# PSUM banks of the attention stage granted one by one, with new engine orders

## The chip, the cores and the metric

The kernel runs on one NeuronCore of one Trainium2 chip. The metric is the device time of one execution in microseconds (us), taken over several runs. The profile comes from one further execution.

## The reference

What has to be computed, in three parts that feed one another (the constants are those of this case):

```python
# q, k, v: (2 batches, 12 heads, 448 tokens, 64)
scores = q @ k.T / 8;  scores = where(above the diagonal, -1e9, scores)
e = exp(scores - rowmax(scores));  attn = e / (rowsum(e) + 1e-9)
x = (attn @ v) laid out as (896 tokens, 768)
h = x @ w_in                                   # 768 -> 2048
g = where(h > 0, h, exp(min(h, 0)) - 1)
y = g @ w_out                                  # 2048 -> 768
m = max(y @ w1, y @ w2, y @ w3)                # 768 -> 768 each
out = m @ w_out2                               # 768 -> 768
```

## The kernel before

The kernel has an attention stage (lines 137 to 573) and three dense stages (line 575 on). In the dense stages weights arrive as 64-bit numbers, are converted and split into a high and a low part by ACT and DVE, and each product is made of three fp32r matmuls.

Attention works on pairs of heads, 12 pairs numbered 0 to B (hexadecimal); pairs 0 to 5 are the first batch. A head's 448 tokens are four chunks of 112. Causality is used: chunk c is scored against the first c+1 chunks only. The stage is written as short steps, and each engine has a list of them in PLAN (lines 436 to 484). A step is a letter and its numbers, pair first:

- **SP:** L loads q and k of a pair, V loads v, R loads a panel of w_in.
- **PE:** Q transposes q (Q.0) or k (Q.1) of a pair, four 112-column transposes into one bank. S computes scores (three steps a pair: S.0 is chunk 3; S.1 is chunks 2 and 0; S.2 is chunk 1), both heads at once, head 0 on the upper 64 rows of the array and head 1 on the lower 64, so it takes two banks. T transposes normalized exponentials of one head (three steps a head: T..0 two transposes, T..1 and T..2 four each). A multiplies by v for both heads of a pair, 64 columns of the array each, into one bank. D is one of six parts of the first dense product for the first batch, panels f = 0 and 1, brought forward as filler.
- **DVE:** M adds the mask, takes the row's negative maximum and writes the scores to SBUF (frees the S bank). I inverts the sums. K copies a Q bank out, C copies a T bank out, Y takes the low part of x out of the A bank. b, c, l, f, k serve the early dense panels.
- **ACT:** E is the exponential with its sum. X writes the high part of x from the A bank. K and C steps stand in whichever list holds them (on_act, line 541). a, h, e, g serve the early dense panels.
- **POOL:** N multiplies an exponential by the inverse.

A loop (lines 555 to 572) walks all lists and issues a step once everything in NEEDS (lines 495 to 521) and the former users of its bank have been issued. It decides only the order in which the program is written; on the chip every engine runs its own list in order and waits on semaphores. The whole stage is under `tc.manual_schedule()`, so the lists are the orders.

PSUM has eight banks. Before, they are three fixed groups, and `bank` hands them out in rotation within the group:

```python
BANKS = {"s": 4, "t": 3, "x": 1}          # line 143
n = turn[kind]
turn[kind] = (n + 1) % BANKS[kind]
return ps_a.tile([P, 512], F32, tag=f"{kind}{n}", name=name)
```

S and the D product take from "s", Q and T from "t", A has the one "x" bank, and so A of pair p also waits for Y of pair p-1 (line 507). `holds` (line 524) lists, for each step that takes a bank, the steps that read it out.

Before the first q arrives, `spin` (line 428) runs eight bf16 matmuls on a tile of zeros, and five more after Q01. When the lists are empty, the attention pools are closed and the dense stage begins at line 584 with panel 0, second batch.

Of the kernel before, what the change touches and what calls it, by code (L numbers as in the profile page):

```python
# [29 lines left out]
def tile_attention_elu_maxout(  # L30
# [112 lines left out]
    BANKS = {"s": 4, "t": 3, "x": 1}  # L143
    turn = dict.fromkeys(BANKS, 0)

    def bank(kind, name):
        n = turn[kind]
        turn[kind] = (n + 1) % BANKS[kind]
        return ps_a.tile([P, 512], F32, tag=f"{kind}{n}", name=name)
# [24 lines left out]
    def qk_pe(p, w):  # L174
        n = nat_t.pop(("qk"[w], p))
        t = bank("t", f"t{'qk'[w]}{p}")
        for c in range(NCH):
            nc.tensor.transpose(  # L178
                t[:, c * C : (c + 1) * C],
                n[:, c].rearrange("p h d -> p (h d)"),  # L180
                ident[:C, :C],
            )
        ps_now["qk", p, w] = t
        if (p, w) == (0, 1):
            spin(5)
# [21 lines left out]
    def s_pe(p, g):  # L207
        grp = GROUPS_S[g]
        o0 = EOFF[grp[0]]
        s = [bank("s", f"s{2 * p + j}_{g}") for j in range(2)]  # L210
# [60 lines left out]
    def t_pe(p, j, g):  # L271
        h = 2 * p + j
        e = e_t[h]
        grp = GROUPS_T[g]
        t = bank("t", f"te{h}_{g}")
        n = 0
        for j in grp:
            for c in range(j, NCH):
                nc.tensor.transpose(  # L279
                    t[:C, n : n + C],  # L280
                    e[:, EOFF[c] + j * C : EOFF[c] + (j + 1) * C],
                    ident[:C, :C],
                )
                n += C
        ps_now["t", h, g] = t[:C, :n], slice(TOFF[grp[0]], TOFF[grp[0]] + n)
# [12 lines left out]
    def av_pe(p):  # L298
        vn = nat_t.pop(("v", p))
        et = [et_t.pop(2 * p + j) for j in range(2)]  # L300
        a = bank("x", f"av{p}")
# [100 lines left out]
    def d_pe(f, part):  # L402
        if part == 0:
            early["ps", f] = bank("s", f"ph{f}_0")
            early["gen", f] = h_products(f, HALVES[0], early["ps", f], parts=KD)
# [22 lines left out]
    def spin(n):  # L428
        for _ in range(n):
# [23 lines left out]
            I00 M213 M203 M113 M103 C012 M200 M210 M202 M212 C000 C002 I11 M312 M201 M310 M211
            I10 M302 M300 K41 K40 I21 C111 M301 M311 M303 M313 I20 C101 b0 M410 C110 C100 Y0 I30
            M400 M412 M402 M403 K51 C201 M413 C212 I31 b1 M401 Y1 M502 M411 M510 M512 M500 K71
            M511 M501 K70 I41 M503 M513 I40 C310 C312 c1 M613 Y2 K80 M602 M600 M603 M612 I50
            M610 C401 M601 I51 M611 C412 M701 M711 C410 Y3 M712 M710 M700 I61 M702 M703 M713 I60
            c0 C510 KA0 M811 M801 M813 M803 Y4 C601 I70 I71 M802 M810 M812 M910 KB1 M902 C610
            M800 M912 M900 C700 KA1 I81 C701 M913 M903 b2 M911 M901 Y5 I80 MA10 KB0 MA12 MA00
            MA13 MA03 MA02 Y6 MA01 I91 C801 C812 MA11 MB13 MB03 I90 l0 MB01 C811 Y7 MB11 MB10  # L460
            IA0 MB12 IA1 l1 C900 C901 Y8 C902 C911 IB1 CA00 MB00 Y9 MB02 CA10 IB0 CB10 YA CB00
            c2 f1 YB k1 f0 k0 l2
# [15 lines left out]
            N212 N211 N201 N203 N202 N210 N301 N302 N200 N303 N300 N312 N311 N313 N310 N412 N411
            N403 N400 N413 N401 N402 N410 N503 N500 N510 N501 N502 N513 N512 N511 N612 N603 N602
            N600 N613 N611 N610 N601 N701 N703 N710 N713 N702 N711 N712 N700 N813 N810 N812 N811  # L480
            N802 N803 N801 N800 N913 N910 N911 N912 N901 N902 N903 NA02 NA01 NA10 N900 NA11 NA03
            NA00 NB11 NA13 NA12 NB12 NB13 NB03 NB02 NB10 NB01 NB00
# [24 lines left out]
        av_pe: lambda p: [(load_v, p), (x_lo, p - 1)] + [(t_copy, p, *t) for t in T_OF],  # L507
# [39 lines left out]
    with tc.manual_schedule():  # L547
# [3 lines left out]
        idle = bank("x", "idle")  # L551
# [4 lines left out]
        while any(waiting):  # L556
            before = len(issued)
            for line in waiting:
                while line:
                    f, args = line[0]  # L560
                    held = [
                        ((kind, (turn[kind] + n) % BANKS[kind]), by)
                        for n, (kind, by) in enumerate(holds(f, args))
                    ]
# [3 lines left out]
                    busy.update(held)  # L568
                    f(*args)
# [328 lines left out]
```

## Time and profile before

| | us |
|---|---|
| median of 3 runs | 502.40 (502.22 to 502.74) |
| the profiled execution | 502.88 |
| its span, first to last instruction | 501.0 |
| PE busy in the span | 495.5 |
| DVE busy | 349.4 |
| ACT busy | 252.8 |
| POOL busy | 52.9 |

PE is TensorE's matmuls, PEld its weight loads, DVE is VectorE, ACT is ScalarE, POOL is GpSimd. Matmuls overlap in the profile: a matmul's row lasts until its result is out, while the next has begun, so PE's busy time is no measure of how tightly it is fed. The chain of waits tells that better: it cuts the time into pieces from the end of one group of instructions to the end of the next.

### The profile page before, as it was taken

The page shows a single profiled execution, that of the slowest core. Times are in us where ns is not written, and L with a number is a line of the kernel's source. Part 1 is how long each engine was busy: PE and PEld are TensorE (multiplying, and loading weights), DVE is VectorE, ACT ScalarE, POOL GpSimd, SP SyncE. Part 2 cuts the span into 40 slices and gives each one's busy share as a digit, 9 for nine tenths or more (in the row PEclk, how much of TensorE's full clock was granted, in tenths as well). Part 3 has the DMA queues.
Part 4 walks back from the last instruction along what each step waited for, and adds up shares of the span by engine and source line. Part 5 has one row for each costly group of instructions (what it writes and reads, how often), then busy time and mean ns, then how long its engine had stood idle before and what let it go on. Part 6 is the DMA issues. An engine that isn't in the chain of part 4 may idle for free.

```text
span 501.0 us, 7404 instructions
## 1 busy us (share of the span) xinstructions
PE 495.5 (99%) x2758; PEld 426.1 (85%) x2758; DVE 349.4 (70%) x707; ACT 252.8 (50%) x523; POOL 52.9 (11%) x104
## 2 busy tenths in 40 slices
PE   9999999999999999999999999999999999999997
PEld 5676666789998889989889989998889999889997
DVE  3999899469977786656556555428997968714793
ACT  4999999667666665543233323224452434202630
POOL 1665566300000000000000000000000000000000
PEclk9999999999999999999999999999999999999999
DMA  9998300026623321132442344305765253000013
GB/s 184 246 238 191 87 18 20 3 63 189 188 77 115 105 79 63 69 126 85 127 126 85 126 113 161 127 0 168 229 233 188 75 179 127 0 1 0 33 63 127
DMA packets 75460, 55.53 MB, mean 111 GB/s; under 512 B 34464, under 2 KB 74656, under 8 KB 75424
## 3 DMA queue, kind: packets, MB, share of 16 engines
q1 hardware_dynamic: 74496, 54.83, 38.3%
q8 instruction: 22, 0.36, 0.3%
q10 hardware_dynamic: 928, 0.23, 0.2%
q14 instruction: 14, 0.11, 0.1%
HBM read 52.30 MB, written 2.75 MB: 110 GB/s over the span
## 4 chain that ended last, share of the span: by engine, by line
PE 97%; POOL 2%; issue 0%; ACT 0%; DVE 0%
PE pm L339 26%; PE ph L339 23%; PE py L630 23%; PE x L761 7%; PE s L216 5%; PE te L279 5%; PE av L304 4%; POOL e L269 2%; PE l L761 1%; PE tk L178 1%; PE tq L178 1%; PE idle L430 1%; ACT o L860 0%; DVE still L550 0%
## 5 line engine op out<-in xcount | busy, mean ns | idle before, releaser
L339 PE MATMUL pm<-yT,ws_m 128*128 128x384 f32 (+1 forms) x648 | 130.4, 362 | 0.0
L339 PEld LDWEIGHTS pm<-yT,ws_m 128*128 128x128 f32 x648 | 117.2, 188 | 13.0
L339 PE MATMUL ph<-xT,ws_l 128*128 128x512 f32 (+2 forms) x576 | 118.2, 364 | 0.0
L630 PE MATMUL py<-gs,ws_o 128*128 128x512 f32 (+1 forms) x576 | 116.2, 363 | 0.0
L339 PEld LDWEIGHTS ph<-xT,ws_l 128*128 128x128 f32 x576 | 104.0, 188 | 12.3 <-issue 1.0
L630 PEld LDWEIGHTS py<-gs,ws_o 128*128 128x128 f32 x576 | 104.3, 188 | 11.7
L269 POOL TENSOR_SCALAR e<-e,r 112x336 f32<-112x336 f32 (+3 forms) x96 | 51.5, 556 | 43.0 <-DVE r L263 11.9
L250 ACT ACTIVATE e<-e,nm 112x448 f32<-112x448 f32 (+3 forms) x96 | 49.6, 524 | 3.4 <-DVE nm L236 3.3
L236 DVE CUSTOM_DVE_ANT_0 e<-s,mask 112x336 f32<-112x336 f32 (+3 forms) x96 | 38.1, 442 | 3.0 <-PE s L216 2.7
L103 ACT ACTIVATE c_m<-raw_m 128x768 f32<-128x768 f32 x24 | 21.9, 913 | 27.1 <-DVE ws_m L131 14.9
L130 ACT ACTIVATE ws_o<-c_o 128x512 fp32r<-128x512 f32 x24 | 15.1, 628 | 34.6 <-PE py L630 34.6
L109 DVE SCALAR_TENSOR_TENSOR c_m<-c_m,raw_m 128x768 uint32<-128x768 uint32 x24 | 22.9, 954 | 12.8 <-ACT c_m L103 12.5
L130 ACT ACTIVATE ws_m<-c_m 128x768 fp32r<-128x768 f32 x18 | 15.2, 846 | 31.3 <-PE pm L339 17.4
L279 PE MATMUL te<-ident,e 112*112 112x112 f32 x240 | 30.1, 263 | 0.9 <-POOL e L269 0.7
L279 PEld LDWEIGHTS te<-ident,e 112*112 112x112 f32 x240 | 23.8, 133 | 8.2 <-POOL e L269 3.7
L103 ACT ACTIVATE c_o<-raw_o 128x512 f32<-128x512 f32 x24 | 16.0, 665 | 26.7 <-DVE ws_o L131 24.1
L130 ACT ACTIVATE gs<-g 128x512 fp32r<-128x512 f32 (+2 forms) x30 | 17.2, 573 | 21.1 <-DVE g L355 21.0
L216 PE MATMUL s<-qk 64*112 64x336 f32 (+3 forms) x192 | 27.8, 416 | 0.0
L131 DVE TENSOR_TENSOR ws_o<-c_o,ws_o 128x512 fp32r<-128x512 f32 x24 | 16.5, 687 | 13.8 <-ACT ws_o L130 13.7
L304 PE MATMUL av<-et,vn 112*64 112x448 f32 (+3 forms) x192 | 25.3, 405 | 0.0
L109 DVE SCALAR_TENSOR_TENSOR c_o<-c_o,raw_o 128x512 uint32<-128x512 uint32 x24 | 16.6, 692 | 11.8 <-ACT c_o L103 11.5
L104 DVE TENSOR_SCALAR raw_o<-raw_o 128x512 uint32<-128x512 uint32 x24 | 10.3, 428 | 20.8 <-DMA raw_o<-in_moe_w_out_dram 20.8
(96 smaller groups left out, 570.1 us busy)
## 6 DMA issues: line engine op xcount, KB each, us to landing
raw_m<-in_moe_w_dram SPq DMA_DIRECT2D x18, 768.0 KB, 4.2
raw_l<-in_moe_w_in_dram SPq DMA_DIRECT2D x16, 768.0 KB, 4.7
raw_o<-in_moe_w_out_dram SPq DMA_DIRECT2D x24, 512.0 KB, 3.5
raw_m<-in_moe_w_out_dram SPq DMA_DIRECT2D x6, 768.0 KB, 4.2
qn<-in_q_dram SPq DMA_DIRECT2D x24, 112.0 KB, 3.8
vn<-in_v_dram SPq DMA_DIRECT2D x12, 224.0 KB, 3.7
out_dram<-o SPq DMA_DIRECT2D x14, 192.0 KB, 1.9
kn<-in_k_dram SPq DMA_DIRECT2D x22, 112.0 KB, 3.8
```

The lines of the kernel that those rows point to most:

```text
L103: nc.scalar.activation(f32(r), f32(high), AF.Copy, scale=BIAS),
L109: nc.vector.scalar_tensor_tensor(r, r, 3, low, ALU.logical_shift_left, ALU.bitwise_or)
L130: nc.scalar.activation(hi, src, AF.Copy)
L216: nc.tensor.matmul(s[j][:C, o : o + (c + 1) * C], qk[:, a, c * C : (c + 1) * C], qk[:, c2, : (c + 1) * C], start=(w == 0 and n == 0), stop ...
L236: nc.vector.tensor_tensor_reduce(out=e_t[h][:, EOFF[c] : EOFF[c] + (c + 1) * C], in0=ps_now.pop(("s", h, c)), in1=mask[:, (NCH - 1 - c) * ...
L250: nc.scalar.activation(e, e, AF.Exp, bias=nm_t[h][:, c : c + 1], scale=-1.0, accum_out=sm_t[p][:, j, c : c + 1],)
L269: nc.gpsimd.tensor_scalar(e, e, ps_now["r", h][:, c : c + 1], 1.0, ALU.mult, ALU.mult)
L279: nc.tensor.transpose(t[:C, n : n + C], e[:, EOFF[c] + j * C : EOFF[c] + (j + 1) * C], ident[:C, :C],)
L304: nc.tensor.matmul(a[j * D : (j + 1) * D, kc * C : S], vn[:, j * NCH + kc, :], et[j][:, TOFF[kc] : TOFF[kc] + S - kc * C], start=(n == 0), ...
L339: nc.tensor.matmul(ps, w(a, kc), x(c, kc), start=(i == 0), stop=(i == len(seq) - 1))
L630: nc.tensor.matmul(py[b][:, : at.stop - at.start], w[:, a, kc * P : (kc + 1) * P], g_sp[hk * HK + kc][:, c, at], start=(hk == 0 and i == 0 ...
L761: nc.tensor.matmul(out, a[:, x, i0 + k, rows], b[:, y, k, :], start=begin and n == 0, stop=end and n == len(seq) - 1,)
```

## The change

`bank` takes the number of the next bank from a list `granted`; the three groups are gone. Every PE step that takes a bank carries its numbers in PE's list behind a colon (an S step two, one for each head), and the loop appends them to `granted` when it issues the step. The former users of that bank, whatever they were, have to be issued first. A now holds its bank until X and Y of its pair, and no longer needs Y of the pair before. All four engine lists are in a new order; eight C steps go from ACT to DVE; K00 goes to DVE, and K01, KB0 and KB1 to ACT, among others, so that ACT holds 14 of the 24 K steps in place of 12. SP's list is the same. The diff, with the lists of DVE and POOL left out:

```diff
--- before.py
+++ after.py
@@ -140,13 +140,10 @@
     nat = attn.enter_context(tc.tile_pool(name="nat", bufs=2))
     hd = attn.enter_context(tc.tile_pool(name="hd", bufs=2))
     ps_a = attn.enter_context(tc.tile_pool(name="ps_a", bufs=1, space=PSUM))
-    BANKS = {"s": 4, "t": 3, "x": 1}
-    turn = dict.fromkeys(BANKS, 0)
-
-    def bank(kind, name):
-        n = turn[kind]
-        turn[kind] = (n + 1) % BANKS[kind]
-        return ps_a.tile([P, 512], F32, tag=f"{kind}{n}", name=name)
+    granted = []
+
+    def bank(name):
+        return ps_a.tile([P, 512], F32, tag=f"b{granted.pop(0)}", name=name)
 
     nat_t, qk_t, e_t, nm_t, et_t, sm_t, ps_now = ({} for _ in range(7))
 
@@ -173,7 +170,7 @@
 
     def qk_pe(p, w):
         n = nat_t.pop(("qk"[w], p))
-        t = bank("t", f"t{'qk'[w]}{p}")
+        t = bank(f"t{'qk'[w]}{p}")
         for c in range(NCH):
             nc.tensor.transpose(
                 t[:, c * C : (c + 1) * C],
@@ -207,7 +204,7 @@
     def s_pe(p, g):
         grp = GROUPS_S[g]
         o0 = EOFF[grp[0]]
-        s = [bank("s", f"s{2 * p + j}_{g}") for j in range(2)]
+        s = [bank(f"s{2 * p + j}_{g}") for j in range(2)]
         for w, (a, c2) in enumerate(PASSES):
             for n, c in enumerate(grp):
                 o = EOFF[c] - o0
@@ -272,7 +269,7 @@
         h = 2 * p + j
         e = e_t[h]
         grp = GROUPS_T[g]
-        t = bank("t", f"te{h}_{g}")
+        t = bank(f"te{h}_{g}")
         n = 0
         for j in grp:
             for c in range(j, NCH):
@@ -298,7 +295,7 @@
     def av_pe(p):
         vn = nat_t.pop(("v", p))
         et = [et_t.pop(2 * p + j) for j in range(2)]
-        a = bank("x", f"av{p}")
+        a = bank(f"av{p}")
         for n, kc in enumerate((0, 1, 3, 2)):
             for j in range(2):
                 nc.tensor.matmul(
@@ -401,7 +398,7 @@
 
     def d_pe(f, part):
         if part == 0:
-            early["ps", f] = bank("s", f"ph{f}_0")
+            early["ps", f] = bank(f"ph{f}_0")
             early["gen", f] = h_products(f, HALVES[0], early["ps", f], parts=KD)
         next(early["gen", f])
         if part == KD - 1:
@@ -438,48 +435,52 @@
             L0 L1 L2 L3 V0 V1 R0 L4 R1 L5 V2 L6 V3 L7 V4 L8 V5 L9 R2 V6 LA V7 LB V8 V9 VA VB
             """,
         "PE": """
-            Q00 Q01 S01 S00 Q11 Q10 S02 Q21 Q20 S12 S11 Q31 Q30 S20 S10 T010 T012 T011 S21 T002
-            T000 T001 S22 S31 A0 Q41 Q40 T111 S32 S30 T112 T102 T101 T110 S41 S40 T100 Q50 T211
-            Q51 T201 A1 Q60 T202 T212 T302 S42 S51 T200 T210 Q61 Q70 T311 Q71 S52 S50 A2 T310
-            T312 T301 T300 S60 S61 Q81 Q80 T411 T401 A3 S62 S72 T400 T412 T402 T410 S70 S71 T502
-            Q91 T500 A4 S82 S80 T510 T511 T501 QA0 T512 T611 Q90 T601 T612 S81 S91 T600 QB1 T602
-            T610 A5 T700 QA1 T701 T711 S90 S92 T710 T712 T702 QB0 SA1 SA0 A6 T810 T800 T801 SA2
-            SB0 T812 T802 T811 A7 SB2 SB1 D00 T900 T912 T901 A8 D10 T910 T902 T911 TA01 D01 TA00
-            TA02 A9 D11 TA12 TA10 TA11 D12 TB10 AA D13 TB12 TB00 D14 TB02 TB01 TB11 D15 D02 AB
-            D03 D04 D05
+            Q00:0 Q01:1 S02:23 S00:45 S01:67 Q11:0 Q10:1 Q21:3 Q20:2 S11:46 S12:01 S10:57 S22:32
+            S20:41 S21:05 Q31:7 Q30:3 T001:2 T002:4 T000:7 T010:5 T012:3 T011:1 S32:75 S31:34
+            S30:12 A0:6 Q40:0 T100:2 Q41:3 T101:1 T111:4 T110:5 T112:0 T102:2 S42:37 S40:14
+            S41:50 A1:2 T202:7 Q50:1 T201:5 Q51:0 Q61:3 T211:4 T210:5 T212:2 Q60:7 T200:3 T312:5
+            T310:1 Q71:0 T300:2 T311:6 T301:4 T302:1 S52:32 S60:75 S61:60 S51:32 S50:41 A2:5
+            A3:2 T410:4 Q81:6 Q70:7 T402:1 T412:0 T400:5 T401:3 T411:6 S62:75 S72:14 S71:36
+            S70:75 A4:0 D00:4 T610:1 Q90:2 T511:6 D01 T512:0 T510:7 Q80:6 T611:5 T612:2 D02
+            QA0:3 Q91:1 T500:0 D03 T600:7 T501:6 T502:3 T601:0 T602:7 S82:21 S81:30 S92:67
+            S91:12 S90:57 S80:63 A5:0 A6:6 D04 T700:5 D05 T711:3 T710:7 T712:0 T702:2 QB0:5
+            QB1:6 T701:7 T802:4 T810:5 QA1:0 T812:7 T801:2 T811:6 T800:5 SB2:04 SA2:32 SB0:16
+            SA0:74 SB1:32 SA1:05 A7:1 A8:4 D10:7 T900:3 T902:0 T901:6 D11 T912:2 T910:0 T911:3
+            D12 TB01:6 A9:0 D13 D14 D15 TB02:2 TB00:3 TB10:4 TA02:5 TA01:1 TA00:2 TB12:4 TB11:6
+            TA11:3 TA12:7 TA10:4 AB:6 AA:2
             """,
         "DVE": """
...
             """,
         "ACT": """
-            K00 E000 E010 E012 K11 K10 E002 E013 E011 K20 E001 E003 K31 E100 E111 K30 E213 C010
-            C011 E113 E110 E210 E112 C001 E101 E102 E103 E212 E202 E211 E300 E203 E201 X0 E200
-            C112 E302 C102 E303 E301 E312 K50 E311 C211 E313 E310 E410 E400 X1 K60 E412 C302
-            C202 a1 C200 C210 K61 E402 E403 E411 E413 E510 E500 C311 E401 E513 E501 C301 E511 X2
-            C300 E502 K81 E503 E512 a0 C411 E603 E613 E600 C400 X3 C402 E602 E610 E611 E612 E711
-            E601 E712 C500 E701 E710 C502 K91 E702 E713 C511 C501 C512 C611 K90 X4 E700 E703
-            C612 E811 C600 E801 E812 E813 C602 E803 E902 E900 E810 C711 X5 E800 C710 E802 E903
-            C702 E913 C712 E911 h1 E910 E912 X6 C800 C810 EA13 E901 EA01 EA03 h0 EA02 C802 EA00
-            EA12 X7 EA10 EA11 EB13 C912 EB10 EB03 EB11 X8 C910 EB01 EB12 a2 CA02 CA01 EB00 X9
-            CA12 CA11 EB02 XA CB12 CB02 CB01 CB11 e1 g1 XB h2 e0 g0
+            K01 E011 E001 E003 E000 K10 E002 K21 K20 E013 E010 E012 E101 E111 E100 E113 K31 K30
+            E103 C010 C012 C011 E212 E102 E210 E110 E112 E202 E200 E203 E213 C100 E211 E201 C101
+            C111 E311 E310 E300 E313 E302 E301 E410 E312 E303 X0 X1 C201 C202 E413 K50 C212 C211
+            a0 K60 C312 C311 K71 E411 E412 C302 E403 E401 E400 h0 E402 E500 E511 E613 E510 X2
+            E600 E501 E512 K81 E513 C402 C401 E610 E612 C412 E611 E602 E503 X3 E502 E601 X4 E603
+            a1 C511 K90 E712 C610 E701 C512 E703 h1 C500 E713 K91 C601 C602 E711 E710 C611 E801
+            E702 E800 E901 E700 E811 E812 E802 E803 E810 X5 E813 E913 E912 X6 e0 a2 KB0 C701
+            E911 KB1 C802 C801 C811 E910 C812 E900 g0 E903 EB11 E902 EB03 EA11 EA01 EA03 EB01
+            EB00 EB02 EA02 EA10 EB12 EA00 X8 EB13 EB10 C912 EA13 EA12 X7 e1 CB10 CB00 CB11 g1 X9
+            CA11 CA01 XB XA h2
             """,
         "POOL": """
...
             """,
     }
 
@@ -504,7 +505,7 @@
         e_norm: lambda p, j, c: [(r_inv, p, j)],
         t_pe: lambda p, j, g: [(e_norm, p, j, c) for c in range(min(GROUPS_T[g]), NCH)],
         t_copy: lambda p, j, g: [(t_pe, p, j, g), (av_pe, p - 2)],
-        av_pe: lambda p: [(load_v, p), (x_lo, p - 1)] + [(t_copy, p, *t) for t in T_OF],
+        av_pe: lambda p: [(load_v, p)] + [(t_copy, p, *t) for t in T_OF],
         x_hi: lambda p: [(av_pe, p)],
         x_lo: lambda p: [(x_hi, p)],
         d_load: lambda f: [],
@@ -523,23 +524,26 @@
 
     def holds(f, args):
         if f is qk_pe:
-            return [("t", [(qk_copy, *args)])]
+            return [[(qk_copy, *args)]]
         if f is t_pe:
-            return [("t", [(t_copy, *args)])]
+            return [[(t_copy, *args)]]
+        if f is av_pe:
+            return [[(x_hi, *args), (x_lo, *args)]]
         if f is s_pe:
             p, g = args
-            return [("s", [(s_max, p, j, c) for c in GROUPS_S[g]]) for j in range(2)]
+            return [[(s_max, p, j, c) for c in GROUPS_S[g]] for j in range(2)]
         if f is d_pe and args[1] == 0:
-            return [("s", [(d_max, args[0])])]
+            return [[(d_max, args[0])]]
         return []
 
-    plan = {
-        e: [(STEP[w[0]], tuple(int(d, 16) for d in w[1:])) for w in line.split()]
-        for e, line in PLAN.items()
-    }
+    def step(word):
+        word, _, at = word.partition(":")
+        return STEP[word[0]], tuple(int(d, 16) for d in word[1:]), [int(d) for d in at]
+
+    plan = {e: [step(w) for w in line.split()] for e, line in PLAN.items()}
 
     def on_act(f, *args):
-        return (f, args) in plan["ACT"]
+        return (f, args, []) in plan["ACT"]
 
     def issued_all(needs):
         return all(x in issued for x in needs if min(x[1:]) >= 0)
@@ -548,7 +552,8 @@
 
         still = const.tile([P, 512], BF16, name="still")
         nc.vector.memset(still, 0.0)
-        idle = bank("x", "idle")
+        granted.append(7)
+        idle = bank("idle")
         spin(8)
 
         issued, busy = set(), {}
@@ -557,15 +562,13 @@
             before = len(issued)
             for line in waiting:
                 while line:
-                    f, args = line[0]
-                    held = [
-                        ((kind, (turn[kind] + n) % BANKS[kind]), by)
-                        for n, (kind, by) in enumerate(holds(f, args))
-                    ]
+                    f, args, at = line[0]
+                    held = list(zip(at, holds(f, args), strict=True))
                     needs = NEEDS[f](*args) + [x for b, _ in held for x in busy.get(b, [])]
                     if not issued_all(needs):
                         break
                     busy.update(held)
+                    granted.extend(at)
                     f(*args)
                     issued.add((f, *args))
                     line.pop(0)
```

## Rows read from the trace of the kernel before

**Rows 1.** The page: span, busy time by engine, granted TensorE clock by slice.

```profile
span 501.0 us, 7404 instructions
...
PE 495.5 (99%) x2758; PEld 426.1 (85%) x2758; DVE 349.4 (70%) x707; ACT 252.8 (50%) x523; POOL 52.9 (11%) x104
...
PEclk9999999999999999999999999999999999999999
```

**Rows 2.** Busy time by stretch: length, then PE, PEld, DVE, ACT, POOL, PE clock, DMA.

```profile
0.00:104.00 104.00, 101.93 (x771) 68.22 (x772) 81.75 (x310) 86.38 (x269) 52.86 (x104) 1.00 0.60 126
...
101.70:140.00 38.30, 38.30 (x192) 34.71 (x191) 32.56 (x48) 26.33 (x44) 0.00 (x0) 1.00 0.45 136
140.00:498.00 358.00, 357.60 (x1810) 325.32 (x1808) 236.56 (x353) 141.46 (x214) 0.00 (x0) 1.00 0.33 105
```

**Rows 3.** Chain that ended last, in order of time, from us 0: start, length, what.

```profile
4.78 0.91 PE tq L178 x4
5.69 0.56 PE tk L178 x4
6.25 1.08 PE idle L430 x5
...
9.03 0.53 PE tk L178 x4
9.56 0.38 PE tq L178 x4
9.95 0.56 PE s L216 x4
...
11.43 1.32 PE s L216 x12
...
13.67 1.71 PE s L216 x8
...
16.57 0.95 PE s L216 x8
...
19.95 2.04 PE av L304 x16
21.99 0.53 PE tk L178 x4
...
81.52 0.80 PE ph L339 x3
...
87.48 0.62 PE ph L339 x3
...
101.76 58.41 PE ph L339 x288
```

**Rows 4.** Waits of the weight loads before 104 us: total, times, longest.

```profile
PEld te L279 <- POOL e L269: 3.7, 8, 0.7
...
PEld te L279 <- ACT e L250: 0.7, 1, 0.7
```

**Rows 5.** ACT groups before 104 us: busy, mean ns, idle before.

```profile
L250 ACT ACTIVATE e<-e,nm 112x448 f32<-112x448 f32 (+3 forms) x96 | 49.6, 524 | 3.4 <-DVE nm L236 3.3
L294 ACT ACTIVATE et<-te 112x448 f32<-112x448 f32 (+1 forms) x42 | 19.8, 491 | 4.6 <-PE te L279 4.6
L250 ACT ACTIVATION_READ_ACCUMULATOR e<-e,nm 112x1 f32 x96 | 18.9, 197 | 0.0
L315 ACT ACTIVATE xT<-av 128x448 fp32r<-128x448 f32 x12 | 6.5, 540 | 3.2 <-PE av L304 3.0
L193 ACT ACTIVATE qk<-tq 128x448 f32<-128x448 f32 x7 | 3.8, 538 | 3.0 <-PE tq L178 3.0
L384 ACT ACTIVATE c_l<-raw_l 128x768 f32<-128x768 f32 x3 | 2.8, 919 | 0.0
L193 ACT ACTIVATE qk<-tk 128x448 f32<-128x448 f32 x5 | 2.7, 538 | 0.2 <-PE tk L178 0.2
L395 ACT ACTIVATE ws_l<-c_l 128x768 fp32r<-128x768 f32 x3 | 2.5, 836 | 0.0
```

**Rows 6.** DVE groups before 104 us, columns as in Rows 5.

```profile
L296 DVE COPY et<-te 112x448 f32<-112x448 f32 (+1 forms) x30 | 15.2, 514 | 1.6 <-PE te L279 0.9
...
L321 DVE TENSOR_TENSOR xT<-av,xT 128x448 fp32r<-128x448 f32 x12 | 7.4, 620 | 6.3 <-ACT xT L315 6.2
...
L110 DVE SCALAR_TENSOR_TENSOR c_l<-raw_l,c_l 128x768 uint32<-128x768 uint32 x3 | 3.2, 1077 | 0.1
...
L109 DVE SCALAR_TENSOR_TENSOR c_l<-c_l,raw_l 128x768 uint32<-128x768 uint32 x3 | 2.8, 942 | 0.0
L398 DVE TENSOR_TENSOR ws_l<-c_l,ws_l 128x768 fp32r<-128x768 f32 x2 | 2.0, 1003 | 0.0
```

**Rows 7.** Busy time by stretch while attention runs, columns as in Rows 2.

```profile
8.40:38.60 30.20, 30.18 (x244) 20.55 (x240) 28.36 (x125) 29.14 (x98) 16.20 (x32) 1.00 1.18 238
38.60:53.10 14.50, 14.28 (x116) 9.58 (x114) 13.36 (x52) 13.82 (x47) 9.46 (x16) 1.00 0.66 150
53.10:63.90 10.80, 10.29 (x87) 7.19 (x86) 9.05 (x30) 9.80 (x32) 5.43 (x9) 1.00 0.36 97
56.40:60.90 4.50, 3.99 (x36) 3.25 (x34) 3.49 (x11) 3.50 (x10) 3.42 (x7) 1.00 0.74 191
```

More of the change, by code (lines that the diff above doesn't have):

```diff
@@ L450, in tile_attention_elu_maxout @@
+            S91:12 S90:57 S80:63 A5:0 A6:6 D04 T700:5 D05 T711:3 T710:7 T712:0 T702:2 QB0:5
[3 more added lines that the diff above has]
+            TA11:3 TA12:7 TA10:4 AB:6 AA:2
             """,
         "DVE": """
-            K01 M000 M010 M012 M002 M003 M013 M001 M011 K21 M111 M101 I01 M102 M100 M112 M110
@@ L453, in tile_attention_elu_maxout @@
[L453 to L462, printed above, removed]
+            K00 M011 M001 M003 M000 M002 K11 M010 M013 M012 I00 M102 M100 M111 M101 M103 M113
+            I01 M201 M211 M203 M212 M210 M213 C000 M110 C002 C001 M112 M202 M200 I10 M302 M310
@@ new lines, in tile_attention_elu_maxout @@
+            M313 M300 I11 M303 M312 M311 K40 K41 M301 I21 I20 C110 C112 C102 b0 M400 M410 M411
+            M403 M402 M412 I31 M401 I30 M413 Y1 K61 C210 K51 Y0 C310 C200 C300 c0 M501 M511 C301
+            M600 M613 M500 M510 M512 I41 M503 I40 M602 M603 M610 M513 M612 Y2 M502 b1 K70 C400
+            C410 C411 M601 M611 I51 M710 M702 I61 l0 M711 M701 Y3 I50 M712 Y4 M703 I60 M713 M700
+            c1 C510 K80 KA0 C600 C612 C502 C501 M811 M801 M800 M810 M911 M901 M802 M812 I71 I70
+            M803 M903 M813 I80 M910 M913 Y5 M912 I81 C700 Y6 C710 M902 f0 C712 C702 C810 KA1
@@ L463, in tile_attention_elu_maxout @@
+            C711 M900 l1 MB11 MA01 MA11 MB01 C800 MB03 MA13 I90 I91 k0 MB00 MA03 MB02 MA00 MA02
+            MA10 MB13 IB0 MB12 MB10 C902 C900 C901 IA0 C910 C911 IB1 Y8 MA12 Y7 IA1 b2 CB02 CB01
+            f1 CB12 CA00 CA10 CA02 CA12 k1 Y9 YB YA c2 l2
             """,
         "ACT": """
-            K00 E000 E010 E012 K11 K10 E002 E013 E011 K20 E001 E003 K31 E100 E111 K30 E213 C010
-            C011 E113 E110 E210 E112 C001 E101 E102 E103 E212 E202 E211 E300 E203 E201 X0 E200
-            C112 E302 C102 E303 E301 E312 K50 E311 C211 E313 E310 E410 E400 X1 K60 E412 C302
@@ L475, in tile_attention_elu_maxout @@
+            a1 C511 K90 E712 C610 E701 C512 E703 h1 C500 E713 K91 C601 C602 E711 E710 C611 E801
[3 more added lines that the diff above has]
+            CA11 CA01 XB XA h2
             """,
         "POOL": """
-            N013 N011 N012 N010 N002 N001 N003 N000 N113 N112 N100 N111 N101 N110 N102 N103 N213
@@ L478, in tile_attention_elu_maxout @@
[L478 to L482, printed above, removed]
+            N001 N002 N003 N000 N012 N010 N013 N011 N101 N103 N102 N111 N112 N113 N110 N100 N201
@@ L483, in tile_attention_elu_maxout @@
+            N200 N211 N203 N212 N210 N202 N213 N311 N312 N303 N310 N313 N302 N300 N301 N412 N411
+            N413 N403 N402 N401 N410 N400 N510 N512 N613 N511 N612 N513 N500 N611 N610 N503 N600
+            N603 N601 N602 N502 N501 N712 N702 N701 N710 N703 N713 N803 N802 N711 N700 N813 N801
+            N810 N812 N800 N811 N911 N901 N910 N903 N900 N913 N902 N912 NB01 NB02 NB00 NB03 NA02
+            NB13 NA03 NA00 NB10 NB12 NA01 NA13 NB11 NA10 NA12 NA11
             """,
```

## The prediction

> **What bounds the kernel now.** First the page: PE is busy for 495.5 of 501.0 us, every other engine far less, and the granted clock is full (2.4 GHz) in every slice [rows 1]. Then the windows, to see in which stage PE could gain. After attention PE has no gap: 38.30 of 38.30 us and 357.60 of 358.00 [rows 2]. Nothing in the dense stages is touched, so what the change is worth is the amount by which the dense stage starts earlier. In attention the window says 101.93 of 104 us for PE, with ACT at 86.38, DVE at 81.75 and POOL at 52.86 [rows 2]. That looks full too, but a matmul's row runs on after the next has begun, so I turn to the chain, whose pieces end where a group of matmuls ends [rows 3].
>
> The chain gives the price of each step, and it shows a price for changing from one kind of matmul to another:
>
> - Four transposes after transposes take 0.38 us (at 9.56), after an S or an A step 0.53 (at 9.03 and 21.99). A run of transposes so costs 0.15 more when it follows S or A.
> - One S.2 step alone takes 0.56 (9.95), one S.1 step alone 0.95 (16.57), but the two in one run 1.32 (11.43). So each run of S steps costs 0.19 over its work. Without it a pair's S.2 and S.1 are 1.13, and S.0 is half of 1.71 less 0.19 (13.67), 0.76: 1.89 a pair.
> - An A step takes 2.04.
> - Three D matmuls take 0.62 after transposes, 0.80 after S or A, and in the dense stage 58.41/288 x 3 = 0.61 [rows 3]. So 0.2 more after S or A.
>
> With these I take the stage before apart. It lasts from 4.78 (the first transpose) to the first dense matmul after D05, which is 101.76 and nine matmuls of 0.203 later plus 0.1 for following an A: 103.7, so 98.9 us. Its work: 12 A x 2.04 = 24.5; 96 + 240 = 336 transposes x 0.096 = 32.2; 12 pairs of S x 1.89 = 22.7; 12 D x 0.61 = 7.3. Together 86.7. The start costs 1.8 on top: the first eight transposes take 1.47 instead of 0.77 and the five idle matmuls 1.08 [rows 3]. PE's old list has 19 runs of S (3.6 us), 20 runs of Q and T that follow an S or A (3.0) and 5 of D that follow an S or A (1.0): 7.6 us of changes. That sums to 96.1. The 2.8 left of the 98.9 are stalls; 3.7 us of waits of weight loads for POOL's normalized exponentials, in eight places, are their face [rows 4].
>
> **The change, part by part.**
>
> *PE's order.* The new list has the same 156 steps. I count 8 runs of S in place of 19, 5 runs of Q and T behind S or A in place of 20, and 4 of D behind an A plus the first dense product behind the last A, 5 as before. Changes then cost 8 x 0.19 + 5 x 0.15 + 5 x 0.2 = 3.3 in place of 7.6: 4.3 us less. This is PE's own time, hidden by nothing.
>
> Four A steps now follow an A directly (A2 A3, A5 A6, A7 A8, AB AA), which the trace does not show. S, transposes and D lose 0.15 to 0.2 when the step before is of their kind, so A may lose between 0 and 0.2 of its 2.04; I take the middle, 0.4 us in all. The Trainium skill (TensorEngine Tiling (Array Packing), Tiling Modes) says that a change of tiling mode drains TensorE while a change of tile does not. S uses half the rows of the array, A half the columns, so by that rule the full 0.8 would go, and the sum would be 0.4 lower; no row here shows two A steps together.
>
> Without stalls the new stage would end at 4.78 + 1.8 + 86.7 + 3.3 - 0.4 = 96.2.
>
> *The banks.* Giving them out costs no instruction. What it allows is the order: six S banks in the first run, T banks beyond three. What it can cost is a wait on a bank whose reader is late. So the question is which engine cannot keep up with a PE that needs 96.2 us.
>
> *ACT and DVE.* Eight C steps go from ACT to DVE and two K steps net come back. At 15.2/30 = 0.51 a C and 0.61 a K, DVE gains 2.8 us [rows 6] and ACT loses about as much. DVE at 85 and ACT at 83 us in all fit into 96; the tight place is the middle. From 8.4 to 53.1 ACT was busy 42.96 of 44.7 us, 96%, then 91% [rows 7], so ACT was close to a bound already. I check the place where the new lists press hardest: S82 takes banks 2 and 1, and bank 1 was Q91's, which K91 on ACT empties. K91 is the 101st step of ACT. Ahead of and with it, after K01 at the very start, stand 60 E, 20 C, 11 K, 5 X, 2 a and 2 h. By the rows: 60 x (49.6 + 18.9)/96 = 42.8, 20 x 0.47 = 9.4, 11 x 0.54 = 5.9, 5 x 0.54 = 2.7, 1.8 and 1.7, together 64.3 [rows 5]. ACT's instructions overlap: all groups before 104 us sum to 108.9 without the table load of 1.3, where the engine was busy for 85.1 [rows 2, 5], so I scale by 0.78: 50.2 us. S02 now comes first, so the first E starts near 8.4. Without a gap ACT is through K91 at 58.6. PE, by the prices above, comes to S82 at 57.8: 12 S steps, 7 A, 8 D and 112 transposes with their changes are left, 38.4 us of the 96.2. So PE is 0.8 late at least; at ACT's 96% it is 2.8 late, at 91% 5.9. A lateness there also serves what follows: to CA01, the last C that AA needs, ACT has 36 E, 14 C and 12 others left, 31 us by the same count, and at 96% is done some 3 us before AA. I take 2.5 us of stalls in all, near the rate of most of the stretch, with ends of 0.8 and 6.
>
> The start is as tight for DVE (S10, S22, S20, S21 each wait for M steps of the pair before), but a lateness there is part of the same sum: PE waits once, and ACT's place at S82 is behind it.
>
> *SP's queue.* Its list is the same. A load of q and k waits for the Q steps four pairs back, one of v for the A five back. The new PE list brings the late Q and A steps forward in their stage, which lets the loads behind them start earlier too; they fall where the DMA engines have room (a share of 0.66 after 38.6 us, 0.36 after 53.1, against 1.18 before [rows 7]). I cost this at nothing; a load that is late would cost the 1 us or so by which it misses its Q step.
>
> *Hand-over to the dense stage.* It now starts right behind AA. Its first product reads pairs 6 to B in turn; pair A's columns come after 12 matmuls, 2.4 us, and X (0.54) and Y (0.62) of A are done in 1.2 [rows 5, 6]. Panel 2's weights are needed after 36 matmuls, 7.3 us; the rest of DVE's list behind YA, c2 (two, 2.0) and l2 (1.0), is done about 4.2 us after AA. Both are hidden; before, D03 to D05 stood there.
>
> **The sum.** The dense stage starts at 96.2 + 2.5 = 98.7 in place of 103.7, 5.0 us earlier. The profiled execution took 502.9, so 497.9; the median before is 502.4, 0.5 below it, so I predict 497.4. In short: 4.3 from fewer changes, 0.4 from paired A steps, and stalls of 2.5 in place of 2.8.
>
> **Rivals.**
>
> 1. *ACT becomes the bound outright.* If ACT runs at 91% as it did from 53.1 to 63.9 [rows 7], PE is 5.9 late at S82 and the time is 500.8. For it: ACT's 96% was reached with the old order; E steps now come in batches behind M steps. Against it: four fifths of the old stretch ran at 96%, and ACT has 2 to 3 us less work.
> 2. *The clock falls (slower).* The new list has stretches of transposes alone: T202 to T302 is 5.9 us, T711 to T800 4.9, TB02 to TA10 3.6. If the granted clock drops to 1.2 GHz in them, a transpose costs what the first ones cost, 0.91/4 to 0.56/4 instead of 0.38/4 [rows 3]. With these 14.4 us at about twice the time for half of their length, plus the start of what follows, some 8 us are lost: 505. It decides if the clock of those stretches reads below 1.00. Against it: nine steps of transposes alone, from 56.4 to 60.9, ran at 1.00, although PE was busy for 3.99 of 4.50 us only [rows 7]. The Trainium skill (TensorE: Matmul & The Clock Gate, Part 4: PE-mode transpose) speaks for it: transposes, it says, don't count as activity in the way other matmuls do, so that the full clock doesn't come on. The trace so far disagrees, for stretches up to 4.5 us.
> 3. *The gain is given back at the hand-over, or not there.* If DVE and ACT are so late that panel 2 or pair A of x is not ready, PE waits in the dense stage for the first time; 3 us of slack have to be used up first, and 5 more to lose it all: 502.4. The same time results if the change between kinds is no cost of PE but of late data; against that stands that the 0.53 repeats wherever I look.
>
> **Chances.** The forecast 0.60 (495 to 499.5), rival 1 0.23 (499.5 to 501.4), rival 2 0.05, rival 3 0.06, and 0.06 that stalls nearly vanish (below 495). A measurement of this kernel can tell 0.2%, 1.0 us, from no change. Faster is the first two and the last, less a little of rival 1's end: 0.88; same 0.06; slower 0.06. The range of 494.8 to 500.6 goes from 0.6 below the smallest stall with the whole A gain (4.3 + 0.8 + 2.8 - 0.8 = 7.1 less than 502.4, and the scaling of ACT's sum is rough) to just short of rival 1's price.
>
> **What would show it.** Right: the chain after has transposes in long runs at 0.38 for four, S runs of a pair and more at 1.89 a pair, about 8 pieces of S; the dense stage's first piece starts near 98.7 and has the same length; clock 1.00; PE's waits name banks or data that ACT frees, around S82. Wrong: a dense stage with gaps, a clock below 1.00, waits for DVE near the start that are larger than those at S82, or paired A steps that cost more than 2.04.

## The result, and the profile after

| | us |
|---|---|
| median of 6 runs, after | 497.86 (497.46 to 498.73) |
| median of 6 runs, before, beside them | 502.13 (501.76 to 502.74) |
| ratio | 0.9916, 95% interval 0.9903 to 0.9929 |
| the profiled execution, after | 497.46, span 495.7 |

The change made the kernel faster by 4.3 us (the interval says 3.6 to 4.9). The forecast was 497.4 us, with a range of 494.8 to 500.6.

The page after; it answers to [rows 1]:

```profile
span 495.7 us, 7384 instructions
...
PE 489.3 (99%) x2758; PEld 426.7 (86%) x2758; DVE 351.5 (71%) x713; ACT 249.2 (50%) x517; POOL 50.2 (10%) x104
...
PEclk9999999999999999999999999999999999999999
```

The same 2758 matmuls keep PE busy for 6.2 us less, at full clock in every slice. To see where, the chain of the kernel after (start, length, what); it answers to [rows 3]:

```profile
4.60 0.57 PE tq L175 x4
...
29.55 0.38 PE te L276 x4
29.93 0.77 PE tk L175 x8
...
34.79 3.60 PE s L213 x28
38.39 3.92 PE av L301 x32
...
74.56 3.97 PE s L213 x32
78.53 3.92 PE av L301 x32
82.45 0.81 PE ph L336 x3
...
84.22 0.62 PE ph L336 x3
...
90.87 3.45 PE te L276 x36
94.32 3.92 PE av L301 x32
98.25 108.79 PE ph L336 x540
207.04 116.00 PE py L633 x576
323.04 130.20 PE pm L336 x648
```

Four things are to be seen. The pieces are long: 28 or 32 S matmuls in a row, 36 transposes in 3.45 us (0.38 for four), two A steps together. Two A steps cost 3.92 where one alone cost 2.04 [rows 3], so a pair saves 0.16; all four pairs read 3.92. Three D matmuls still cost 0.81 behind an A and 0.62 behind transposes. And the dense part follows without a gap, with ph, py and pm in one piece each: the gain is the earlier start of the piece at 98.25. The first dense matmul starts at 98.18, against 103.62 before.

That is 5.4 us earlier, of which 0.64 is not the change: the first S matmul starts at 6.62 in place of 7.26, because the matmuls ahead of it reach their short length earlier in this execution (the first four transposes take 0.57 here, 0.91 before). This goes with the execution and not with the orders: with the old orders the first S starts at 6.54 in the profile of banks_timed2 and at 7.65 in that of banks_timed, with the new ones at 7.15 in that of first_free (all three below). From the first S to the dense stage it is 96.36 before and 91.56 after: 4.8 us, at the upper end of the 3.6 to 4.9 that the times say. All stage times below are this length, and "stalls" are what it holds beyond the prices of its steps and of the changes between them, as the chain gives them.

### The profile page after: what moved, and what is told of

It is laid out like the page before. It is cut to its first block, busy times and chain, and to the rows that moved or that the text cites. A ratio compares the mean times of both kernels' runs of the same rounds, so it can differ in the third digit from the quotient of the medians.

```text
span 495.7 us, 7384 instructions
## 1 busy us (share of the span) xinstructions
PE 489.3 (99%) x2758; PEld 426.7 (86%) x2758; DVE 351.5 (71%) x713; ACT 249.2 (50%) x517; POOL 50.2 (10%) x104
## 4 chain that ended last, share of the span: by engine, by line
PE 95%; DVE 2%; DMA 2%; issue 0%; POOL 0%; ACT 0%; SPq 0%; DVEq 0%
PE pm L336 26%; PE py L633 23%; PE ph L336 23%; PE x L764 7%; PE s L213 5%; PE av L301 4%; PE te L276 4%; PE l L764 1%; DMA raw_l<-in_moe_w_in_dram 1%; PE tk L175 1%; DVE e L233 1%; DMA qn<-in_q_dram 1%; PE tq L175 1%; POOL e L266 0%; DVE c_l L109 0%
## 5 line engine op out<-in xcount | busy, mean ns | idle before, releaser
L266 POOL TENSOR_SCALAR e<-e,r 112x336 f32<-112x336 f32 (+3 forms) x96 | 48.9, 528 | 41.9 <-DVE r L260 34.1
L233 DVE CUSTOM_DVE_ANT_0 e<-s,mask 112x224 f32<-112x224 f32 (+3 forms) x96 | 37.8, 441 | 2.3 <-PE s L213 2.2
L276 PE MATMUL te<-ident,e 112*112 112x112 f32 x240 | 27.5, 260 | 1.3 <-POOL e L266 1.2
L213 PE MATMUL s<-qk 64*112 64x336 f32 (+3 forms) x192 | 25.3, 405 | 0.3 <-DVE nm L233 0.3
```

Of the source, the lines that this page charges most:

```text
L213: nc.tensor.matmul(s[j][:C, o : o + (c + 1) * C], qk[:, a, c * C : (c + 1) * C], qk[:, c2, : (c + 1) * C], start=(w == 0 and n == 0), stop ...
L233: nc.vector.tensor_tensor_reduce(out=e_t[h][:, EOFF[c] : EOFF[c] + (c + 1) * C], in0=ps_now.pop(("s", h, c)), in1=mask[:, (NCH - 1 - c) * ...
L266: nc.gpsimd.tensor_scalar(e, e, ps_now["r", h][:, c : c + 1], 1.0, ALU.mult, ALU.mult)
L276: nc.tensor.transpose(t[:C, n : n + C], e[:, EOFF[c] + j * C : EOFF[c] + (j + 1) * C], ident[:C, :C],)
```

## The experiments

Four questions: what in the orders gives the gain, whether the banks alone give any, why PE still stalls after, and whether that can be taken away. The kernel before was timed again beside each group of runs: 502.34 (pin4, n_order_pin4, banks_alone, split_a), 502.48 (no_c1, banks_timed, first_free, n_order), 502.63 (the last three).

**The price of changing the kind of matmul: split_a** (here and below, pieces of the lines of PLAN)

```diff
-A5:0 A6:6 D04 T700:5 D05 T711:3
+A5:0 D04 A6:6 D05 T700:5 T711:3
-A7:1 A8:4 D10:7 T900:3 ... D11
+A7:1 D10:7 A8:4 D11 T900:3
```

> The changed kernel with D04 and D05 put around A6, D10 and D11 around A8, so that two of the four pairs of A steps are parted and four D follow an A instead of two; same steps, same banks, in a stretch without stalls. Theory (changes of kind cost PE time): each place loses 0.15 of the paired A, pays 0.1 for A after D and 0.2 for one more D after A: 0.8 to 0.9 us slower than the changed kernel, 498.7. Rival (a change of kind costs nothing once data is there): 497.9.

Measured 498.60 (498.44 to 499.60), ratio 0.9931 (0.9918 to 0.9943); stage 92.55, 0.99 longer. Its chain, beside the pieces of 3.92 and 0.62 above:

```profile
78.92 2.04 PE av L301 x16
80.96 0.81 PE ph L336 x3
81.77 2.04 PE av L301 x16
83.81 0.81 PE ph L336 x3
```

The same steps, in an order that splits two pairs of A and puts two more D steps behind an A, cost more at both places: by the pieces 0.16 for the pair and 0.19 for the D step, 0.35 each, so 0.7 of the 0.99. The other 0.3 lies mostly in the transposes behind A8 (T912 to TB01), which now come sooner to data that isn't ready; no new wait is long enough to be listed. The run times of the two kernels have overlapping intervals; the rows carry this verdict.

**The same for S and transposes: split_s** (against n_order_pin4, which is further down)

```diff
-T102:2 S42:37
+S42:37 T102:2
-T302:1 S52:32
+S52:32 T302:1
-T800:5 SB2:04
+SB2:04 T800:5
```

> n_order_pin4 with three pairs of neighbours exchanged in the PE list (T102 with S42, T302 with S52, T800 with SB2): the same instructions, three more runs of S and three more runs of transposes that follow an S, no wait that a trace of n_order_pin4 lets expect above 0.1 us. Theory (a change of kind costs TensorE time by itself): 3 x (0.19 + 0.15) = 1.0 us more than n_order_pin4, 497.3 us, with no new wait listed. Rival (changes of kind are free and the gain is shorter waits): 496.2 to 496.5 us.

Measured 496.66 (496.32 to 497.27), ratio 0.9880 (0.9866 to 0.9893), beside 496.25 and 0.9877 (0.9864 to 0.9891) for n_order_pin4: by time these can't be told apart, and the expected 497.3 was missed. The trace says why. The chain of split_s at the first two places:

```profile
24.07 0.59 PE s L213 x4
24.66 0.53 PE te L276 x4
25.18 1.70 PE s L213 x12
...
34.43 0.57 PE s L213 x4
35.00 0.53 PE te L276 x4
35.52 3.21 PE s L213 x24
```

Four transposes between two S runs read 0.53. From T112 to S40, four steps, it is 2.436 us in place of 2.081; from T301 to S60 2.414 for 2.080; from T811 to SA2 1.864 for 1.533. That is 0.355 + 0.334 + 0.331 = 1.02 us, the expected price. But the stage grew by 0.58 only: small stalls at T202, Q61, S71 and S70, 0.48 in all in n_order_pin4, are 0.06 in split_s. PE came 0.35 later to steps that had been waiting for data, and the wait shrank by what the change of kind had cost. So the price is real, and it is paid in full only where PE doesn't wait anyway.

**The banks alone: banks_alone and banks_timed.** Both keep the old orders and give all eight banks out freely (A no longer waits for the Y before); the numbers differ. banks_alone takes the bank that was free first in the order in which the program is written; banks_timed takes it by the times in the trace of before.

```diff
-    BANKS = {"s": 4, "t": 3, "x": 1}
+    granted = []
-            Q00 Q01 S01 S00 Q11 Q10 S02 ...
+            Q00:0 Q01:1 S01:23 S00:45 Q11:6 Q10:7 S02:01 ...   # banks_timed
```

> Old lists of all engines, eight free banks (each step takes the bank that was taken longest ago and is free), so the banks alone. Theory (the gain is fewer changes of matmul kind in PE's order): no gain, 502.1 within 0.5. Rival (the gain is that no step waits for a bank of its group): most of the 4.3 us come, 498 to 499.

> Old lists again with eight banks, but every bank number written out: the bank that was free longest by the times in the trace of the kernel before, so that no step waits for a bank there. Theory (gain from the order, not from the banks): 502.2 within 0.5. Rival (waits for banks of a group were what the old kernel lost): 498 to 500.

Measured: banks_alone 506.74 (506.63 to 508.29), ratio 1.0097 (1.0082 to 1.0111), stage 100.68 with 7.4 us of stalls in place of 3.1. banks_timed 505.68 (503.93 to 506.22), ratio 1.0058 (1.0044 to 1.0072). Neither was expected slower: theory and rival both failed. In banks_alone, PE waits for readers of the banks it was given:

```profile
PE av L301 <- DVE nm L233: 1.2, 1, 1.2
PE tq L175 <- DVE xT L318: 1.0, 1, 1.0
...
PE s L213 <- DVE xT L318: 0.7, 1, 0.7
PE te L276 <- DVE xT L318: 0.6, 1, 0.6
```

An A bank is free only after X and Y (xT), and an order written on paper doesn't know when these run. In banks_timed the stalls inside attention fell to 2.4, but at the hand-over the first dense product was given the bank of the D product just ended. Its wait, and the windows behind it (length, PE, PEld, DVE, ACT, POOL, PE clock, DMA):

```profile
PE ph L336 <- DVE g L352: 1.9, 1, 1.9
```

```profile
105.70:109.20 3.50, 3.50 (x11) 3.10 (x10) 1.49 (x2) 0.21 (x1) 0.00 (x0) 0.51 0.00 0
109.20:120.00 10.80, 10.80 (x54) 9.70 (x53) 7.21 (x11) 6.98 (x12) 0.00 (x0) 1.00 0.13 32
```

After 1.9 us of idling, the granted clock read 0.51 (the level of 1.2 GHz) for 3.5 us: 11 matmuls there, where the next 10.8 us hold 54. At their rate 11 take 2.2, so the wait of 1.9 cost 1.3 more in this execution. It was not so in all: of the six runs three have a mean granted clock of 0.997, as the profiled one, and took 506.15 to 506.22; the other three have 1.000 and took 503.93 to 505.21.

**The banks alone, without that wait: banks_timed2**

```diff
-            ... Q10:7 ... S12:46 S11:57 ... D00:7 ... TB12:4 ...
+            ... Q10:4 ... S12:76 S11:54 ... D00:4 ... TB12:7 ...   # 4 and 7 exchanged everywhere
```

> The orders of the kernel before with all eight banks given out by numbers, as in banks_timed, but with banks 4 and 7 exchanged in every step, so that the dense stage's first product no longer waits for the product that fills the last stage of attention. Theory (order: the gain is fewer changes of kind on TensorE, and the freely given banks are only what lets such an order run): the waits of attention that a later free bank set fall by 0.7 us, as banks_timed showed, and nothing else moves: 502.4 - 0.7 = 501.7 us, 501.2 to 502.4. Rival (banks: free banks are themselves the gain, and banks_timed hid it behind its 1.9 us at the hand-over and the lower clock after it): 498 to 500 us.

Measured 502.25 (501.08 to 502.88, 11 runs) beside 502.63 (15 runs), ratio 0.9989 (0.9981 to 0.9998): 0.1 to 1.0 us faster, as the order theory said, and nowhere near 498 to 500. Stage 96.03, stalls 2.8. It is 3.4 us below banks_timed, most of it the wait and, in half of the runs there, the clock after it. Freely given banks are worth 0.3 (by the stage) to 0.5 us (by the times) with the old orders; the rest of the gain needs the new ones.

**Could the order do without chosen banks? first_free.** The new orders, with each bank given as in banks_alone:

```diff
+                    free = [b for b in banks if issued_all(busy.get(b, []))][: len(asked)]
...
-                    granted.extend(at)
+                    granted.extend(free)
```

> New lists as in the changed kernel, banks by program order (the one taken longest ago whose readers are issued) in place of the written numbers. If the numbers matter as the slower of the two kernels with old lists suggests, A banks that Y frees late fall to steps that come soon: 2 to 6 us of new stalls, 500 to 504. If any free bank will do with the new lists: 497.9.

Measured 513.64 (512.49 to 513.89), ratio 1.0218 (1.0205 to 1.0231); stage 105.99, stalls 17.6. The direction is as expected; the size is well beyond it, and the cause is another. For Y (xT), which was expected, PE waits 1.2 us in all; most is for M steps (nm) that free S banks, at seven places for A and transposes alone, and for C steps on ACT (3.2):

```profile
PE te L276 <- DVE nm L233: 3.1, 4, 1.6
PE av L301 <- DVE nm L233: 2.1, 3, 0.9
```

Some 1 us of the time goes with a lower clock: the profiled run has a mean granted clock of 1.000 and took 512.49, the other three have 0.993 to 0.997 and took 513.6 to 513.89.

Worked out on the lists and not run: with three fixed groups the new orders can't be written down at all; however eight banks are split, the issuing loop comes to a step whose bank is only freed by a later one.

**The stalls that are left: POOL beside c1.** PE's waits after, which answer to [rows 4] (there of the weight loads):

```profile
PE te L276 <- POOL e L266: 1.2, 1, 1.2
PE s L213 <- DVE nm L233: 0.3, 1, 0.3
PE tq L175 <- DMA qn<-in_q_dram: 0.2, 1, 0.2
```

The first is T500, 1.33 us late, waiting for N502, which stands in POOL's list behind N601 and N602. POOL's groups from 53.1 to 55.7 (busy, mean ns), and DVE's in the same stretch:

```profile
L266 POOL TENSOR_SCALAR e<-e,r 112x336 f32<-112x336 f32 x1 | 1.2, 1237 | 0.0
L266 POOL TENSOR_SCALAR e<-e,r 112x224 f32<-112x224 f32 x1 | 1.2, 1167 | 0.0
```

```profile
L109 DVE SCALAR_TENSOR_TENSOR c_l<-c_l,raw_l 128x768 uint32<-128x768 uint32 x1 | 1.5, 1461 | 0.0
L110 DVE SCALAR_TENSOR_TENSOR c_l<-raw_l,c_l 128x768 uint32<-128x768 uint32 x1 | 1.1, 1091 | 0.0
```

Theory: while DVE runs the two instructions of c1, POOL's N stand still. Rival: PE is simply a little ahead of DVE and ACT there, and T500 is where it shows. no_c1 leaves out c1's two instructions (panel 1's weights are only half converted):

```diff
-        early["w", f] = conv_last(*early.pop(("c", f)))
+        low, r, high = early.pop(("c", f))
+        early["w", f] = f32(r) if f == 1 else conv_last(low, r, high)
```

> The changed kernel without the two DVE instructions of c1 (panel 1 of w_in stays half converted, so part of the first dense product is wrong). Theory (c1, whose operands lie in SBUF, blocks POOL's N601 and N602 and so makes T500 late): N601 and N602 take 0.45 and 0.55 us in place of 1.17 and 1.24, the wait of 1.2 us for POOL at T500 goes, and since panel 4's load starts earlier without c1 the 0.9 us before the S steps of pairs 8 and 9 go as well: 496. Rival (ACT is late there): the two N keep their length, or T500 keeps its wait; 497 to 498.

Measured 495.87 (495.61 to 496.21), ratio 0.9869 (0.9856 to 0.9882); stage 89.68, stalls 1.3. POOL's groups from 51 to 58 in it:

```profile
L266 POOL TENSOR_SCALAR e<-e,r 112x224 f32<-112x224 f32 x3 | 1.4, 467 | 0.0
...
L266 POOL TENSOR_SCALAR e<-e,r 112x336 f32<-112x336 f32 x2 | 1.1, 567 | 0.0
```

The 224 columns take 0.47 in place of 1.17, the 336 columns 0.57 in place of 1.24: 1.37 us less, which is T500's 1.33. The Trainium skill (SBUF — State Buffer, Who interferes with whom) states that a DVE instruction with two SBUF inputs contends with a GpSimd instruction that reads SBUF. c's instructions have two inputs in SBUF and N reads SBUF, and this trace agrees. Before, c0 did the same to N603 and N602 (1.19 and 1.24 us, from 54.9 to 57.4).

The whole trace of the kernel after says the same. Of its 96 N only six take more than 1.12 times the usual length of their shape, and all six run beside a DVE step of the early dense panels that works in SBUF alone: N601 and N602 beside c1, N613 beside l0 (1.16 for 0.64), N911 beside k0 (0.64 for 0.45), N211 beside b0 (1.19 for 0.45) and NA13 beside b2 (0.76 for 0.64). A b step has one input in SBUF, not two, so two inputs aren't the whole condition. N211 and b0 in the rows of POOL and DVE from 25.9 to 26.5:

```profile
L266 POOL TENSOR_SCALAR e<-e,r 112x224 f32<-112x224 f32 x1 | 1.2, 1193 | 0.0
L385 DVE TENSOR_SCALAR raw_l<-raw_l 128x768 uint32<-128x768 uint32 x1 | 0.6, 551 | 0.0
```

By itself no_c1 doesn't exclude that 2.6 us less of DVE work helped; n_order takes nothing away.

**Another order of N: n_order**

```diff
 DVE   -K70 C400 C410 C411 M601 M611 I51 M710
       +K70 I51 C400 C410 C411 M601 M611 M710
 POOL  -N510 N512 N613 N511 N612 N513 N500 N611 N610 N503 N600 N603 N601 N602 N502 N501
       +N510 N512 N511 N513 N613 N612 N611 N610 N500 N503 N502 N600 N603 N601 N602 N501
```

> The changed kernel with I51 earlier and N502 ahead of pair 6 alone, the shift of panel 4 left where it was. Theory (two separate stalls): the 1.3 us at T500 shrink to some 0.3, the 0.9 at S92 to S80 stay: 496.9 to 497.1. Rival (one lateness that shows at either place): nothing gained, 497.9.

Measured 498.04 (497.77 to 498.21), ratio 0.9913 (0.9899 to 0.9927): nothing gained. The wait for POOL is gone from the list, and another has grown:

```profile
PE s L213 <- DVE nm L233: 1.5, 1, 1.5
```

In the kernel after, the same place, S92 to S80, costs 0.9. What PE waits for there is in the chain of after:

```profile
54.52 1.10 DVE c_l L110
55.62 0.02 SPq L93
55.65 0.04 issue
55.69 4.67 DMA raw_l<-in_moe_w_in_dram
...
60.46 0.06 DVE raw_l L104
60.52 0.42 issue
60.94 0.22 DVE e L233
```

raw_l is panel 4's weights of the dense stage. Its buffer comes free when c1 ends at 55.6; the load lands 4.7 us later. The shift of these weights (line 104) is no step of any list: it belongs to the dense stage, is not kept in program order from the third turn of its loop on (f = 2, line 593), and stood in DVE's queue ahead of M811, where it waited for the load. The load lands at a time that c1 sets, so a PE that is earlier at T500 waits longer at S92. The two waits are one after the other, and the second takes what the first gives back.

**The shift kept in its place: pin4 and n_order_pin4**

```diff
-                        split_win(i, f"l{i}", f < 2)
+                        split_win(i, f"l{i}", f < 3)
```

> The first shift of panel 4's weights, which DVE meets in the middle of attention in the changed kernel and which there waits for its load, is kept behind attention. Theory (the remaining stalls are a DVE waiting for that load before the S steps of pairs 8 and 9, and a POOL blocked by c1 ahead of T500): the 0.9 us of PE stalls at S92 to S80 go, 497.9 becomes 497.0. Rival (ACT is the bound, as forecast): ACT is late there anyway, 497.9 stays within 0.2.

> As pin4, and POOL gets pair 5's I51 earlier in DVE's list and multiplies N502 ahead of the N steps of pair 6. No step is added or dropped. Theory: T500 no longer waits for POOL, another 1.3 us go: 495.7. Rival (ACT is the bound): T500 or S82 waits for ACT instead, about 497.

Measured: pin4 497.02 (496.70 to 497.11), ratio 0.9892 (0.9878 to 0.9905), stage 90.84: the stall at S92 is gone, that of T500 stays (1.36). n_order_pin4 496.25 (495.84 to 496.62), ratio 0.9877 (0.9864 to 0.9891), stage 89.87, stalls 1.45, and no wait is listed for PE after the warm-up. It beats both kernels. In it POOL's two N beside c1 are as slow as before (1.15 and 1.24 us); only no PE step stands behind them.

**A last try: best**

```diff
-T202:7 Q50:1 T201:5 Q51:0 Q61:3 T211:4 T210:5 T212:2      (PE)
+T202:7 Q50:1 T201:5 Q51:0 T211:4 T210:5 Q61:3 T212:2
-K70 I51 C400 C410 C411 M601                                (DVE)
+K70 C400 C410 C411 I51 M601
```

I51 moves by three steps, not by the two that the expectation says.

> n_order_pin4 with the inverse I51 two steps later on VectorE and Q61 two steps later on TensorE, aimed at its last two small waits (0.1 to 0.2 us each): 495.9 to 496.2 us. If a wait only moves to the next step, 496.3 us.

Measured 496.55 (496.39 to 496.64), ratio 0.9875 (0.9860 to 0.9890): not told apart from n_order_pin4 by time; its stage, 90.58, is 0.7 longer. With Q61 out of the way PE comes to T211 earlier and is 0.58 late for it, waiting 0.4 for DVE; the wait only moved.

## Why the prediction came out, point by point

- *The place of the gain.* Right: the dense stages are unchanged and without a gap, and the dense stage starts at 98.18 where 98.7 was forecast.
- *Changes of kind, 4.3 us.* Right. With the prices of the chain the same step counts give 4.2, and split_a and split_s show that such a change is PE's own time. "Hidden by nothing" was too much: in split_s 0.4 of the 1.0 came back, because PE then waited less for data. The Trainium skill's rule that a change of tiling mode drains TensorE (TensorEngine Tiling (Array Packing), Tiling Modes) pointed this way, and the trace agrees: two A steps in a row take 3.92, two apart 4.08.
- *Paired A steps, 0.4 between 0 and 0.8.* 0.64, by four pieces of 3.92. 4.2 + 0.64 is the 4.8 us of the stage.
- *Stalls, 2.5 in place of 2.8.* The size was near, 3.1 in place of 3.1, but by luck, since none of it came about as forecast. The place was wrong, and this is the step that failed: "PE is 0.8 late at least" at S82, because of K91 on ACT. ACT did run as full as I took it, and better than the 96% (30.12 + 14.45 of 44.7 us); here are the windows that answer to [rows 7]:

```profile
8.40:38.60 30.20, 30.08 (x264) 22.56 (x262) 29.46 (x128) 30.12 (x102) 16.05 (x32) 1.00 1.09 232
38.60:53.10 14.50, 14.50 (x122) 10.07 (x119) 13.62 (x58) 14.45 (x46) 9.53 (x20) 1.00 0.81 177
53.10:63.90 10.80, 9.30 (x76) 7.51 (x74) 9.13 (x30) 8.74 (x30) 3.87 (x5) 1.00 0.25 76
```

  K91 ended at 58.5, by the sum 58.6. But PE came to S82 at 59.28, held up at T500 by POOL; and with that stall gone, in n_order_pin4, K91 is done at 57.85 and PE comes to S82 at 58.35, so ACT is ahead by half a microsecond. POOL, with half its time free, was the engine I did not check, although [rows 4] names it for 3.7 us of waits before, and ACT for 0.7. The right question was not how busy POOL is, but what stands ahead of the one N that PE needs, and how long each of these takes beside c.
- *Rival 1, ACT the bound.* Did not happen; see above.
- *Rival 2, the clock falls in long runs of transposes.* Did not happen. The longest stretch, T202 to T302, in the window of the kernel after:

```profile
28.62:34.79 6.17, 6.12 (x63) 5.75 (x62) 6.10 (x19) 6.09 (x15) 4.53 (x10) 1.00 0.99 189
```

  Its granted clock is 1.00. The Trainium skill's rule on transposes and the full clock (TensorE: Matmul & The Clock Gate, Part 4: PE-mode transpose) is not borne out here: 6.2 us of transposes and nothing else kept the clock that the S and A steps before them had. Whether the clock would also rise in transposes alone no run here shows. The price of this rival took the first transposes to be at 1.2 GHz, which is read from their length only; no row shows a lower granted clock there.
- *Rival 3, given back at the hand-over.* Did not happen in this kernel; the piece at 98.25 has no gap. banks_timed shows what a wait of 1.9 there costs: that and, in half of the runs, 1.3 for the clock.
- *SP's queue, at nothing.* Nearly: one wait of 0.2 for q (Q61), and the late weight load behind S92, which the part on SP did not think of, since it looked at q, k and v.

What stays open: how much free banks save by themselves in the new orders can't be split off, since these don't run without them.

## What to carry to other kernels

Where PE is the bound and its matmuls are of several shapes, read the chain for what the first of a run costs over the others, and count runs: here 0.15 to 0.2 us each, and 26 fewer of them (11 of S, 15 of transposes) gave most of the gain. When buffers are given out freely, choose them by the times at which their readers are done, those of the stage that follows included; the same freedom with numbers in written order gave kernels 4 and 11 us slower than the fixed groups of before. And when a stall is taken away, look first whether something with a fixed time, such as a load behind the same instruction, stands right after it.

## What the runs showed of the hardware that was not expected

- A GpSimd tensor-by-scalar of 112x224 took 0.47 us alone and 1.17 beside a two-input DVE instruction on 128x768 uint32; one of 112x336 took 0.57 and 1.24. A one-input DVE shift of 128x768 uint32 in SBUF did the same: 1.19 for 112x224 (N211). DVE loses too: its first c instruction took 1.46 us there, 0.94 in the mean of before [rows 6].
- Two A steps in a row took 3.92 us, two with other work between them 4.08.
- A wait of PE of 1.9 us at full clock was followed by 3.5 us at a granted clock of 0.51 in the profile of banks_timed; by their mean clocks, three of its six runs had such a fall and three had none. Waits of 1.2 us (T500 in the kernel after) and 1.5 us (S92 in n_order) were not followed by one: the windows of 1 to 2.5 us around them read 1.00.
